# Queries loaded with eight neighbouring tokens of a head pair on a partition

## The chip, the cores and the metric

The kernel runs on one core of a Trainium2 chip. The metric is the time of one execution on the device in microseconds (us). The version before takes 182.44 us, the median of three runs (182.11 to 183.53). The profile comes from one further execution, which took 183.05 us; the span that its trace covers is 181.3 us.

## The reference

A retention recurrence feeds a multiplicative feed-forward network. There are 4 batches, 8 heads, 768 tokens and a head size of 64; the second part takes the 3072 tokens with the heads side by side, 512 wide.

```python
for t in range(S):                       # q, k, v: (4, 8, 768, 64)
    state = gamma[None, :, None, None] * state + einsum('bhd,bhe->bhde', k[:, :, t], v[:, :, t])
    y[:, :, t] = scale * einsum('bhd,bhde->bhe', q[:, :, t], state)
x = y.transpose(0, 2, 1, 3).reshape(B * S, H * D)   # (3072, 512)
h = (x @ w1) * (x @ w2) @ w3                        # 512 -> 1024 -> 1024
out = h @ w_out                                     # (3072, 512), float32
```

## The kernel before

**Tiles.** The tokens are cut into 12 tiles of 256, three to a batch. In each, the recurrence is computed in parallel form: scores of keys against queries, masked to the causal part, times v, plus the queries times the state that came in. Tiles 0 and 1 (`n < EO`) use one layout, tiles 2 to 11 another one with two blocks of 128 tokens. All matrix products are in float16, with float32 sums.

**Loading.** `load` (line 79) brings one tile of q, k or v into a staging buffer of 128 partitions by 1024 float32; there are 15 such buffers. Queries of all tiles, and k and v of tiles 0 and 1, come in one transfer each with two neighbouring tokens of every head on a partition, so each contiguous row is 2 x 64 x 4 = 512 bytes. k and v of later tiles come as two transfers with rows of 256 bytes. Weights come in rows of 4096 bytes. All transfers are issued by SyncE (SP), in one order: the string of names at line 124 (`r` rows of w3, `wo` of w_out, `w1` and `w2`, and q, k, v by tile), then in the tile loop the transposes of tile n+2 (`turns`), the loads of tile n+3 (`loads`), and stores of finished tiles (`STORES`, line 894). A transpose waits for its cast, and whatever stands behind it on SP waits with it.

**Queries.** `cast` (line 269) rounds a staged tile to float16, mostly on GpSimd (POOL), and orders its columns by token within the partition and then by head and feature. The transpose, by TensorE for the first tiles (`turn`) and by a DMA later (`dma_turn`), gives `qT` of shape (128, 2, 4, 128): the partition is a feature of one of two heads, then come the token's parity, the head pair, and the partition that the token was loaded on. A head pair's columns for 32 partitions are thus two contiguous runs of 32 float16.

**Products.** `scores` (lines 331 and 340) multiplies keys by queries, `inter` (line 434) the incoming state by queries, both as 64 by 64 matmuls in four quadrants of the array. `mask` (lines 351 and 357) applies the causal mask, `av` (line 462) adds the product with v. Query columns are in the order of their layout, the even tokens of a block ahead of the odd ones, and so are the tables `keep`, `YS` and `YN`.

**Out of the recurrence.** `x_out` (lines 474 and 482) multiplies by the decay table on VectorE (DVE) and writes `XT`, in which tokens are in their own order again. It is one operation for the first half of the columns and, from tile 2 on, two of 64 partitions for the second, whose two heads have changed places. Its output pattern puts consecutive results of one parity two float16 apart.

**Feed-forward.** w3 @ w_out is folded into `W3O` at the start (line 256). A tile's `two_blocks` (line 497, line 527 for tiles 0 and 1) multiplies W1 and W2 by `XT`; ScalarE (ACT) copies the first product to `pa`, and VectorE multiplies it by the second into `ht` (line 63, with `pa`). `o_unit` (line 545) multiplies by `W3O`, `o_copy` (line 559) scales on ScalarE.

**Order of the work.** Everything is in one order that is written out by hand; each engine does its instructions in that order. Up to tile 3 the order is a list of calls, from line 585 on, with matmuls on zeros (`warm`, line 578) among the first. From tile 4 on a loop gives, for tile n: inter(n), the fences, the last ht of tile n-1, scores and state products of tile n+1, av(n), x_out(n), states and masks of n+1, transposes of n+2, loads and casts of n+3, the two output rows of n-1, then eight blocks of 8 matmuls, W1 and W2 in turn, over three banks of the accumulator memory (`F2`, `F0`, `F1`). The first block is in F2, the second in F0, and the fifth needs F0 again, after the first ht has read it.

Of the kernel before, what the change touches and what calls it, by code (L numbers as in the profile page):

```python
# [21 lines left out]
def kernel(  # L22
# [11 lines left out]
    nc = tc.nc  # L34
# [44 lines left out]
    def load(nm, n, via=None):  # L79
        via = via or nc.sync  # L80
        b, c = divmod(n, PER)
        t = new_stage()
        src = source[nm][b, :, c * T : (c + 1) * T, :]
        if nm == "q" or n < EO:

            via.dma_start(
                t[:, :].rearrange("p (h x) -> p h x", x=2 * D), src.rearrange("h (p t) d -> p h (t d)", t=2)
            )
        else:
            for s in range(2):  # L90
                via.dma_start(
                    t[:, s * 512 : (s + 1) * 512].rearrange("p (h d) -> p h d", d=D),
                    src[:, s * 128 : (s + 1) * 128, :].rearrange("h i d -> i h d"),
                )
        tok_in[nm, n] = t

    def load_rows(src, i):
        t = new_stage()
        nc.sync.dma_start(t[:, :], src[i * 128 : (i + 1) * 128, :])
        return t  # L100

    def load_wo(i):
# [9 lines left out]
    def fetch(names):  # L112
        for x in names.split():
            kind, i = x[:-1], int(x[-1])
            if kind == "r":
                w3_st[i] = load_rows(moe_w3, i)
            elif kind == "wo":
                wo_st[i] = load_wo(i)
            elif kind in ("w1", "w2"):
                w_st[kind, i] = load_rows({"w1": moe_w1, "w2": moe_w2}[kind], i)  # L120
            else:
                load(kind, i)
# [22 lines left out]
    def numbers():  # L145

        nc.gpsimd.iota(key_i[:, :, :], pattern=[[1, 2], [0, H]], base=1 - 128, channel_multiplier=2)
        nc.gpsimd.iota(
            col_i[:, :, :].rearrange("p g (t j) -> p g t j", t=2), pattern=[[128, 2], [1, 2], [2, 64]],
            base=1 - 128, channel_multiplier=0,  # L150
        )

# [13 lines left out]
    def late_numbers():  # L166

        nc.gpsimd.iota(tok_i[:, :, :], pattern=[[128, 2], [0, H]], base=1 - 128, channel_multiplier=1)
        for g in range(2):
            nc.gpsimd.iota(  # L170
                pos_i[:, g, :, :].rearrange("p s (t i) -> p s t i", t=2), pattern=[[128, 2], [1, 2], [2, 32]],
                base=1 - 128 + 64 * g, channel_multiplier=0,
            )

# [58 lines left out]
    def cast_wo(i, eng):  # L233
        copy(eng, WO[i][:, :, :].rearrange("p a n -> p (a n)"), wo_st[i][:, :])

    def cast_w3(f, eng):
        w3h[f] = att.tile([128, 1024], HP, tag="w3h", name="w3h", bufs=5)
        copy(eng, w3h[f][:, :], w3_st[f][:, :])

    def turn_w3(f, tag):  # L240
        src, ps = w3h.pop(f), bank(tag, [128, 1024], HP)
        for g in range(8):
            c0 = g // 2 * 256 + g % 2
            nc.tensor.transpose(ps[:, g * 128 : (g + 1) * 128], src[:, c0 : c0 + 255 : 2], ident16[:, :])
        w3p[f] = ps

    def turned_w3(f, eng):
        w3t[f] = fsb.tile([128, 1024], HP, tag="pa", name="w3t", bufs=8)
        copy(eng, w3t[f][:, :], w3p.pop(f)[:, :])

    def w3_mm(f, i, tag=None, first=False, last=False):
        if first:
            acc[f] = bank(tag, [128, DM])
        for r in range(2):
            g = 2 * i + r
            nc.tensor.matmul(  # L256
                acc[f][:, :], lhsT=w3t[f][:, g * 128 : (g + 1) * 128], rhs=WO[i][:, r, :],
                start=(first and r == 0), stop=(last and r == 1),
            )

# [8 lines left out]
    def cast(nm, n, eng):  # L269
        dst = {"q": q16, "k": k16}[nm]  # L270
        dst[n] = t = att.tile([128, 2, 512], HP, tag=nm + "16", name=nm + "16", bufs=3)
        src = tok_in.pop((nm, n))
        if nm == "q" or n < EO:
            copy(
                eng, t[:, :, :].rearrange("p t (h d) -> p h t d", d=D),
                src[:, :].rearrange("p (h t d) -> p h t d", t=2, d=D),
            )
        else:
            copy(eng, t[:, :, :].rearrange("p s c -> p (s c)"), src[:, :])
# [37 lines left out]

    QUARTERS = ((0, 0), (1, 1), (0, 1), (1, 0))

    def qchunk(n, r, a, s, g):  # L320
        c = 2 * s + g
        return qT[n][half(r), :, a, c * 32 : (c + 1) * 32]

    def scores(n, tags, hp=None):
        if n < EO:
            ps = [bank(t, [128, 2, 2, 128]) for t in tags]
            for i in range(2):
                for t in range(2):
                    for r, g in QUARTERS:
                        a = hp * 2 + i  # L330
                        nc.tensor.matmul(
                            ps[r][half(g), i, t, :], lhsT=kT[n][half(r), t, a, half(g)],
                            rhs=qT[n][half(r), :, a, half(g)], start=True, stop=True,
                        )
        else:
            ps = [bank(t, [128, NP, 2, 64]) for t in tags]
            for a in range(NP):
                for s in range(2):
                    for r, g in QUARTERS:
                        nc.tensor.matmul(  # L340
                            ps[r][half(g), a, s, :], lhsT=kT[n][half(r), s, a, half(g)],
                            rhs=qchunk(n, r, a, s, g), start=True, stop=True,
                        )
        for r in range(2):
            am[n, hp, r] = ps[r]
# [73 lines left out]
    def inter(n, tags):  # L419
        begun = set()  # L420
        for g in range(2):
            X[n, g] = bank(tags[g], [128, NP, 128])
        cs = chunks(n)
        for a in range(NP):
            for c, r in [(c, r) for c in cs for r in range(2)] if n < EO else [
                ((s, g), r) for s in range(2) for g, r in ((0, 0), (1, 1), (0, 1), (1, 0))
            ]:
                if (n, c) in TS:
                    if n < EO:
                        g, o, rhs = c, X[n, c][half(r), a, :], qT[n][half(r), :, a, half(c)]  # L430
                    else:
                        s, g = c
                        o, rhs = X[n, g][place(n, g, r), a, s * 64 : (s + 1) * 64], qchunk(n, r, a, s, g)
                    nc.tensor.matmul(  # L434
                        o, lhsT=TS[n, c][half(r), a, :], rhs=rhs, start=((g, r) not in begun), stop=False,
                        skip_group_check=True,
                    )
                    begun.add((g, r))
        X[n] = begun
# [28 lines left out]
    def x_out(n, g):  # L468
# [3 lines left out]
        if n < EO:  # L472
            order = "p a (t i) -> p a t i"
            nc.vector.tensor_tensor(  # L474
                XT[n][:, :, g * 128 : (g + 1) * 128].rearrange("p a (i t) -> p a t i", t=2),
                x[:, :, :].rearrange(order, t=2), YS[:, g, :, :].rearrange(order, t=2), MULT,
            )
        else:
            xt = XT[n][:, :, :].rearrange("p a (s x) -> p (a s) x", s=2)[:, :, g * 64 : (g + 1) * 64]
            for to in (slice(0, 128),) if g == 0 else (half(0), half(1)):  # L480
                at = to if g == 0 else slice(64 - to.start, 128 - to.start)
                nc.vector.tensor_tensor(  # L482
                    xt[to].rearrange("p k (i t) -> p k t i", t=2),
                    x[at, :, :].rearrange("p a (s t i) -> p (a s) t i", s=2, t=2),
                    YN[at, g, :, :, :].rearrange("p a s (t i) -> p (a s) t i", t=2), MULT,
                )


# [61 lines left out]

    o_sb = {}

    def o_copy(n, tb, c0=0, c1=512):
        if n not in o_sb:
            if n < LAST:
                o_sb[n] = fsb.tile([128, 2, DM], FP, tag="osb", name="osb", bufs=3)[:, :, :]
            else:
                o_sb[n] = new_stage()[:, :].rearrange("p (t c) -> p t c", t=2)
        nc.scalar.activation(o_sb[n][:, tb, c0:c1], o_ps.pop((n, tb, c0, c1))[:, :], AF.Copy, scale=final_scale)  # L559

    def o_store(n, tb, c0=0, c1=512):
        r0 = n * T + tb * 128
# [2 lines left out]
    def o_store_all(n):  # L565
        nc.sync.dma_start(
            out[n * T : (n + 1) * T, :].rearrange("(t p) c -> p t c", t=2), o_sb[n][:, :, :]
        )

    def o_out(n, tb, cuts=((0, 512),)):  # L570
        for c in cuts:
            o_copy(n, tb, *c)
            o_store(n, tb, *c)

    def warm(m, tag="X1"):
        ps = bank(tag, [128, 512])
# [315 lines left out]
    LATE = ()  # L892

    STORES = {6: (2,), 7: (3,), 8: (4,), 9: (5, 0), 10: (6, 7, 1), 11: (8, 9, 10)}
    TVIA = ()
    for n in range(LAST, NS):
        nxt = n + 1 < NS and n > LAST
        late = nxt and n in LATE
        if n > LAST:
# [16 lines left out]
            o_unit(n - 1, 1, ("F0",))  # L916
            o_copy(n - 1, 1)
            for m in STORES.get(n, ()):
                o_store_all(m)
        else:  # L920
            catch_up()
        tags = ("F2", "F0", "X1" if late else "F1")
# [18 lines left out]
                state(n + 1, 5)  # L941
    cuts = ((0, 320), (320, 512))
    o_unit(NS - 1, 0, ("F2",))
    o_out(NS - 1, 0)
    o_unit(NS - 1, 1, ("F0", "F1"), cuts)
    o_out(NS - 1, 1, cuts)


# [28 lines left out]
```

## Time and profile before

| | us |
|---|---|
| median of 3 runs | 182.44 (182.11 to 183.53) |
| the profiled execution, its own time | 183.05 |
| its span in the trace | 181.3 |
| TensorE busy | 174.7 (96%) |
| VectorE busy | 111.5 (61%) |
| ScalarE busy | 68.1 (38%) |
| GpSimd busy | 53.4 (29%) |
| DMA packets on the hardware queue | 83,552, 40.38 MB, 96.2% of 16 engines |
| granted TensorE clock | 1.00 |

The page gives the busy time of each engine over the whole span and the span in 40 slices of 4.5 us. A line of a group has the code line, the engine, the operation, output and inputs by name, the shape and the count; then the busy time, the mean of one in nanoseconds, the idle time ahead of it and what ended that. A line of the timeline begins with its start and its length in us, and ends with the idle time ahead of it, where there was any. Matmuls overlap, so one takes longer from start to end than the distance to the next. SPq is the queue of SyncE: its lines are issues of transfers, and their lengths include the time for which the issue was held.

### The profile page before, as it was taken

The page shows a single profiled execution, that of the slowest core. Times are in us where ns is not written, and L with a number is a line of the kernel's source. Part 1 is how long each engine was busy: PE and PEld are TensorE (multiplying, and loading weights), DVE is VectorE, ACT ScalarE, POOL GpSimd, SP SyncE. Part 2 cuts the span into 40 slices and gives each one's busy share as a digit, 9 for nine tenths or more (in the row PEclk, how much of TensorE's full clock was granted, in tenths as well). Part 3 has the DMA queues.
Part 4 walks back from the last instruction along what each step waited for, and adds up shares of the span by engine and source line. Part 5 has one row for each costly group of instructions (what it writes and reads, how often), then busy time and mean ns, then how long its engine had stood idle before and what let it go on. Part 6 is the DMA issues. An engine that isn't in the chain of part 4 may idle for free.

```text
span 181.3 us, 5987 instructions
## 1 busy us (share of the span) xinstructions
PE 174.7 (96%) x2615; PEld 124.8 (69%) x2615; DVE 111.5 (61%) x212; ACT 68.1 (38%) x123; POOL 53.4 (29%) x55
## 2 busy tenths in 40 slices
PE   7999989899999999999999999999999999999993
PEld 2454645688965685885867858768688587784872
DVE  7541769785775949549469387484674856836330
ACT  8783555620373231323314314232232231331422
POOL 4101243355403254503445343424414410000000
DMA  5999999999999999999999999999999997200303
GB/s 202 348 413 362 347 323 361 409 365 229 215 218 215 207 210 228 118 231 164 237 219 201 219 157 261 216 167 247 267 168 274 157 407 272 94 26 4 116 0 118
DMA packets 83579, 40.76 MB, mean 225 GB/s; under 512 B 61409, under 2 KB 78049, under 8 KB 83553
## 3 DMA queue, kind: packets, MB, share of 16 engines
q1 hardware_dynamic: 83552, 40.38, 96.2%
q8 instruction: 20, 0.33, 0.8%
q14 instruction: 7, 0.05, 0.1%
HBM read 29.36 MB, written 6.29 MB: 197 GB/s over the span
## 4 chain that ended last, share of the span: by engine, by line
PE 91%; DMA 4%; DVE 2%; ACT 1%; issue 1%; ACTq 0%
PE psF L497 35%; PE psF L545 20%; PE psF L578 5%; DMA st<-in_v_dram 4%; PE psX L256 3%; PE psS L527 2%; PE psS L256 2%; PE psX L527 2%; PE psS L545 2%; PE psX L434 2%; PE psS L497 2%; PE psK L527 2%; PE psF L527 2%; PE psX L462 2%; PE psX L497 1%; PE psS L340 1%
## 5 line engine op out<-in xcount | busy, mean ns | idle before, releaser
L497 PEld LDWEIGHTS <-w 128*128 128x128 f16 x640 | 62.6, 98 | 9.4
L497 PE MATMUL psF<-xt,w 128*128 128x256 f16 x576 | 64.4, 273 | 0.0
L63 DVE TENSOR_TENSOR ht<-pa,psF 128x512 f16<-128x512 f32 x39 | 26.7, 685 | 25.8 <-PE psF L497 25.7
L545 PE MATMUL psF<-w3o,ht 128*128 128x512 f16 (+2 forms) x168 | 36.5, 370 | 0.0
L60 ACT COPY pa<-psF 128x512 f32<-128x512 f32 x37 | 21.7, 586 | 33.8 <-PE psF L497 33.8
L545 PEld LDWEIGHTS <-ht 128*128 128x128 f16 x200 | 18.5, 98 | 19.5
L63 POOL TENSOR_TENSOR v<-st,VN 128x1024 f16<-128x1024 f32 x10 | 19.0, 1904 | 21.6 <-DMA st<-in_v_dram 21.6
L482 DVE TENSOR_TENSOR xt<-psX,YN 64x512 f16<-64x512 f32 (+1 forms) x30 | 21.8, 727 | 3.2 <-PE psX L462 2.6
L559 ACT ACTIVATE st<-psF 128x512 f32<-128x512 f32 (+2 forms) x19 | 10.9, 575 | 31.7 <-PE psF L545 31.7
L60 POOL CAST k<-st 128x1024 f16<-128x1024 f32 x8 | 8.3, 1038 | 25.4 <-DMA st<-in_k_dram 20.9
L527 PEld LDWEIGHTS <-w 128*128 128x128 f16 x128 | 12.4, 98 | 2.1 <-issue 0.5
L60 POOL CAST q<-st 128x1024 f16<-128x1024 f32 x9 | 9.4, 1041 | 9.3 <-DMA st<-in_q_dram 7.1
L578 PE MATMUL psF<-zeros 128*128 128x512 f16 x31 | 10.1, 464 | 1.2 <-DVE zeros L132 1.2
L357 DVE TENSOR_TENSOR am<-psS,keep 128x512 f16<-128x512 f32 x16 | 10.2, 680 | 0.8 <-PE psS L340 0.8
L256 PEld LDWEIGHTS <-w3t 128*128 128x128 f16 x64 | 5.7, 98 | 6.0 <-issue 0.3
L256 PE MATMUL psS<-wo,w3t 128*128 128x512 f16 x32 | 8.5, 379 | 0.0
L63 POOL TENSOR_TENSOR t<-s,GS 128x256 f16<-128x256 f32 x8 | 4.9, 614 | 12.1 <-DVE s L63 10.4
L256 PE MATMUL psX<-wo,w3t 128*128 128x512 f16 x32 | 8.4, 380 | 0.0
L60 DVE COPY fence<-psX 128x8 f32<-128x8 f32 x8 | 1.3, 166 | 11.3 <-PE psX L434 11.3
L578 PEld LDWEIGHTS <-zeros 128*128 128x128 f16 x31 | 3.3, 114 | 5.5 <-issue 3.2
L527 PE MATMUL psS<-xt,w 128*128 128x256 f16 x32 | 6.1, 272 | 0.5 <-DVE xt L474 0.5
L60 POOL CAST w<-st 128x1024 f16<-128x1024 f32 x5 | 5.2, 1041 | 4.5 <-DMA st<-in_moe_w_dram 4.5
(131 smaller groups left out, 199.0 us busy)
## 6 DMA issues: line engine op xcount, KB each, us to landing
st<-in_moe_w_dram SPq DMA_DIRECT2D x16, 512.0 KB, 8.2
st<-in_q_dram SPq DMA_DIRECT2D x12, 512.0 KB, 6.7
st<-in_v_dram SPq DMA_DIRECT2D x20, 256.0 KB, 6.0
st<-in_k_dram SPq DMA_DIRECT2D x20, 256.0 KB, 4.9
out_dram<-st SPq DMA_DIRECT2D x8, 512.0 KB, 5.7
st<-in_moe_w_out_dram SPq DMA_DIRECT2D x4, 512.0 KB, 9.9
out_dram<-osb SPq DMA_DIRECT2D x3, 512.0 KB, 5.7
st<-in_k_dram SPq DMA_DIRECT2D x2, 512.0 KB, 9.6
```

The lines of the kernel that those rows point to most:

```text
L60: {"v": nc.vector.tensor_copy, "g": nc.gpsimd.tensor_copy, "s": nc.scalar.copy}[eng](dst, src)
L63: (nc.vector if eng == "v" else nc.gpsimd).tensor_tensor(dst, a, b, op)
L256: nc.tensor.matmul(acc[f][:, :], lhsT=w3t[f][:, g * 128 : (g + 1) * 128], rhs=WO[i][:, r, :], start=(first and r == 0), stop=(last and r = ...
L357: nc.vector.tensor_tensor(t[:, :, :, :].rearrange("p a s i -> p (a s) i"), ps[:, :, :, :].rearrange("p a s i -> p (a s) i"), keep64[:, :]. ...
L434: nc.tensor.matmul(o, lhsT=TS[n, c][half(r), a, :], rhs=rhs, start=((g, r) not in begun), stop=False, skip_group_check=True,)
L462: nc.tensor.matmul(o, lhsT=v16[n][half(g), t, h * D : (h + 1) * D], rhs=rhs, start=((g, r) not in begun), stop=(n >= EO or t == 1), skip_g ...
L482: nc.vector.tensor_tensor(xt[to].rearrange("p k (i t) -> p k t i", t=2), x[at, :, :].rearrange("p a (s t i) -> p (a s) t i", s=2, t=2), YN ...
L497: nc.tensor.matmul(ps[:, i, :], lhsT=W[d][:, f * 128 : (f + 1) * 128], rhs=XT[n][:, d, :], start=(i == 0 and d == 0), stop=(i == 1 and d = ...
L527: nc.tensor.matmul(rows_ps[w, n, uh][j // 2][:, j % 2, :], lhsT=W[d][:, f * 128 : (f + 1) * 128], rhs=XT[n][:, d, :], start=(first and j % ...
L545: nc.tensor.matmul(ps[:, :], lhsT=HT[n][:, f, tb * 128 : (tb + 1) * 128], rhs=W3O[f][:, c0:c1], start=(f == 0), stop=(f == 7),)
L559: nc.scalar.activation(o_sb[n][:, tb, c0:c1], o_ps.pop((n, tb, c0, c1))[:, :], AF.Copy, scale=final_scale)
L578: nc.tensor.matmul(ps[:, :], lhsT=zeros[:, 0:128], rhs=zeros[:, :], start=True, stop=True)
```

## The change

Queries are loaded by four transfers, one for each head pair `a`. Transfer `a` fills the partitions a, a+4, a+8 and so on, with eight neighbouring tokens of both heads of the pair on each: 2 rows of 8 x 64 x 4 = 2048 bytes. The cast orders the columns by token, then by head of the pair and feature. After the transpose, the 128 columns for one of the eight token places are partitions, with head pairs interleaved: a head pair's columns are every fourth one, in eight groups. `queries` is the pattern that picks them. The number tables, and with them the masks and decays, follow the new order of tokens, and `x_out` undoes eight places instead of two, so that consecutive results are eight float16 apart in `XT`.

The stores of tiles 0, 1 and 2 become two transfers of 256 KB each. The number and order of all instructions on TensorE, VectorE, ScalarE and GpSimd stay as they were. On SyncE there are 39 more, each where its single one was. Some helpers gain arguments that keep their old meaning by default; these are left out here.

```diff
 def load(nm, n, via=None):
...
-        if nm == "q" or n < EO:
+        if nm == "q":
+
+            for a in range(NP):
+                via.dma_start(
+                    t[a::NP, :].rearrange("p (r x) -> p r x", r=2),
+                    src[2 * a : 2 * a + 2, :, :].rearrange("r (p t) d -> p r (t d)", t=8),
+                )
+        elif n < EO:
...
-            col_i[:, :, :].rearrange("p g (t j) -> p g t j", t=2), pattern=[[128, 2], [1, 2], [2, 64]],
+            col_i[:, :, :].rearrange("p g (t j) -> p g t j", t=8), pattern=[[128, 2], [1, 8], [8, 16]],
...
-                pos_i[:, g, :, :].rearrange("p s (t i) -> p s t i", t=2), pattern=[[128, 2], [1, 2], [2, 32]],
+                pos_i[:, g, :, :].rearrange("p s (t i) -> p s t i", t=8), pattern=[[128, 2], [1, 8], [8, 8]],
...
 def cast(nm, n, eng):
-        if nm == "q" or n < EO:
+        if nm == "q":
+            copy(
+                eng, t[:, :, :].rearrange("p x c -> p (x c)").rearrange("p (t r d) -> p r t d", t=8, r=2),
+                src[:, :].rearrange("p (r t d) -> p r t d", r=2, t=8),
+            )
+        elif n < EO:
...
+    def queries(n, r, a, i0, i1):
+
+        x = qT[n][half(r), :, :, :].rearrange("p x a i -> p (x a i)").rearrange("p (t i a) -> p t i a", t=8, a=NP)
+        return x[:, :, i0:i1, a]
+
     def qchunk(n, r, a, s, g):
         c = 2 * s + g
-        return qT[n][half(r), :, a, c * 32 : (c + 1) * 32]
+        return queries(n, r, a, c * 8, (c + 1) * 8)
...
-                            rhs=qT[n][half(r), :, a, half(g)], start=True, stop=True,
+                            rhs=queries(n, r, a, 16 * g, 16 * g + 16), start=True, stop=True,
...
-                        g, o, rhs = c, X[n, c][half(r), a, :], qT[n][half(r), :, a, half(c)]
+                        g, o, rhs = c, X[n, c][half(r), a, :], queries(n, r, a, 16 * c, 16 * c + 16)
...
 def x_out(n, g):
-                XT[n][:, :, g * 128 : (g + 1) * 128].rearrange("p a (i t) -> p a t i", t=2),
-                x[:, :, :].rearrange(order, t=2), YS[:, g, :, :].rearrange(order, t=2), MULT,
+                XT[n][:, :, g * 128 : (g + 1) * 128].rearrange("p a (i t) -> p a t i", t=8),
+                x[:, :, :].rearrange(order, t=8), YS[:, g, :, :].rearrange(order, t=8), MULT,
...
-                    xt[to].rearrange("p k (i t) -> p k t i", t=2),
-                    x[at, :, :].rearrange("p a (s t i) -> p (a s) t i", s=2, t=2),
-                    YN[at, g, :, :, :].rearrange("p a s (t i) -> p (a s) t i", t=2), MULT,
+                    xt[to].rearrange("p k (i t) -> p k t i", t=8),
+                    x[at, :, :].rearrange("p a (s t i) -> p (a s) t i", s=2, t=8),
+                    YN[at, g, :, :, :].rearrange("p a s (t i) -> p (a s) t i", t=8), MULT,
...
+    HALVED = (0, 1, 2)
...
             for m in STORES.get(n, ()):
-                o_store_all(m)
+                if m in HALVED:
+                    o_store(m, 0)
+                    o_store(m, 1)
+                else:
+                    o_store_all(m)
```

More of the change, by code (lines that the diff above doesn't have):

```diff
@@ L95, in load, with load_rows @@
         tok_in[nm, n] = t
-    def load_rows(src, i):
+    def load_rows(src, i, c=0, n=1024):
         t = new_stage()
-        nc.sync.dma_start(t[:, :], src[i * 128 : (i + 1) * 128, :])
+        nc.sync.dma_start(t[:, 0:n], src[i * 128 : (i + 1) * 128, c : c + n])
         return t
@@ L115, in fetch @@
             if kind == "r":
-                w3_st[i] = load_rows(moe_w3, i)
+                w3_st[i, None] = load_rows(moe_w3, i)
+            elif kind[0] == "y":
+                w3_st[int(kind[1]), i] = load_rows(moe_w3, int(kind[1]), 512 * i, 512)
             elif kind == "wo":
@@ L234, in cast_wo, with cast_w3, turn_w3, turned_w3 @@
         copy(eng, WO[i][:, :, :].rearrange("p a n -> p (a n)"), wo_st[i][:, :])
[L236 to L242, printed above, removed]
+    def cast_w3(f, eng, z=None):
+        n = 1024 if z is None else 512
+        w3h[f, z] = att.tile([128, 1024], HP, tag="w3h", name="w3h", bufs=5)
+        copy(eng, w3h[f, z][:, 0:n], w3_st[f, z][:, 0:n])
+    def turn_w3(f, tag, z=None):
+        src, ps = w3h.pop((f, z)), bank(tag, [128, 1024], HP)
+        for g in range(8 if z is None else 4):
             c0 = g // 2 * 256 + g % 2
             nc.tensor.transpose(ps[:, g * 128 : (g + 1) * 128], src[:, c0 : c0 + 255 : 2], ident16[:, :])
[L245 to L249, printed above, removed]
+        w3p[f, z] = ps
+    def turned_w3(f, eng, z=None):
+        n = 1024 if z is None else 512
+        w3t[f, z] = t = fsb.tile([128, 1024], HP, tag="pa", name="w3t", bufs=8)
+        copy(eng, t[:, 0:n], w3p.pop((f, z))[:, 0:n])
     def w3_mm(f, i, tag=None, first=False, last=False):
@@ L254, in w3_mm @@
         for r in range(2):
-            g = 2 * i + r
+            src, g = (w3t[f, None], 2 * i + r) if (f, None) in w3t else (w3t[f, i // 2], 2 * (i % 2) + r)
             nc.tensor.matmul(
-                acc[f][:, :], lhsT=w3t[f][:, g * 128 : (g + 1) * 128], rhs=WO[i][:, r, :],
+                acc[f][:, :], lhsT=src[:, g * 128 : (g + 1) * 128], rhs=WO[i][:, r, :],
                 start=(first and r == 0), stop=(last and r == 1),
@@ L551, with o_copy @@
     o_sb = {}
-    def o_copy(n, tb, c0=0, c1=512):
+    def o_copy(n, tb, c0=0, c1=512, eng="s"):
         if n not in o_sb:
@@ L558, in o_copy @@
                 o_sb[n] = new_stage()[:, :].rearrange("p (t c) -> p t c", t=2)
-        nc.scalar.activation(o_sb[n][:, tb, c0:c1], o_ps.pop((n, tb, c0, c1))[:, :], AF.Copy, scale=final_scale)
+        dst, src = o_sb[n][:, tb, c0:c1], o_ps.pop((n, tb, c0, c1))[:, :]
+        if eng == "s":
+            nc.scalar.activation(dst, src, AF.Copy, scale=final_scale)
+        else:
+            nc.vector.tensor_scalar_mul(dst, src, final_scale)
     def o_store(n, tb, c0=0, c1=512):
@@ L568, in o_store_all @@
         )
[L570 to L573, printed above, removed]
     def warm(m, tag="X1"):
@@ L918 @@
             for m in STORES.get(n, ()):
-                o_store_all(m)
+                if m in HALVED:
+                    o_store(m, 0)
+                    o_store(m, 1)
+                else:
+                    o_store_all(m)
         else:
@@ L943 @@
     o_unit(NS - 1, 0, ("F2",))
-    o_out(NS - 1, 0)
+    o_copy(NS - 1, 0)
+    o_store(NS - 1, 0)
     o_unit(NS - 1, 1, ("F0", "F1"), cuts)
-    o_out(NS - 1, 1, cuts)
+    for c, eng in zip(cuts, "ss"):
+        o_copy(NS - 1, 1, *c, eng=eng)
+        o_store(NS - 1, 1, *c)
 _INS = ['q', 'k', 'v', 'moe_w1', 'moe_w2', 'moe_w3', 'moe_w_out']
```

## The prediction

> **What bounds the kernel now.** I read the page's totals and slices first, then its chain, then the timeline of one tile in the steady part, then the groups by shape, and last the start, where transfers matter.
>
> ```profile
> PE 174.7 (96%) x2615; PEld 124.8 (69%) x2615; DVE 111.5 (61%) x212; ACT 68.1 (38%) x123; POOL 53.4 (29%) x55
> PE   7999989899999999999999999999999999999993
> DMA  5999999999999999999999999999999997200303
> PE 91%; DMA 4%; DVE 2%; ACT 1%; issue 1%; ACTq 0%
> ```
>
> Two rows are full: TensorE to the end, the DMA engines for four fifths of the span. The chain settles which one sets the time: 91% of it is TensorE, 4% a DMA. Making transfers cheaper is therefore worth only what TensorE waits for them. The part that decides is what a tile does on VectorE:
>
> ```profile
> 92.72 0.59 PE L462 MATMUL psX<-am,v 64*64 64x64 f16 x32
> 93.25 3.63 PE L545 MATMUL psF<-w3o,ht 128*128 128x512 f16 x16
> 93.47 2.21 DVE L482 TENSOR_TENSOR xt<-psX,YN 128x512 f16<-128x512 f32 x3 [0.30 <-PE psX L462]
> 95.71 0.42 DVE L60 CAST t<-psK 128x256 f16<-128x256 f32 x1
> 96.71 4.97 PE L497 MATMUL psF<-xt,w 128*128 128x256 f16 x44
> 97.43 1.28 DVE L357 TENSOR_TENSOR am<-psS,keep 128x512 f16<-128x512 f32 x2
> 98.73 0.69 DVE L63 TENSOR_TENSOR ht<-pa,psF 128x512 f16<-128x512 f32 x1
> 100.48 0.69 DVE L63 TENSOR_TENSOR ht<-pa,psF 128x512 f16<-128x512 f32 x1 [1.06 <-PE psF L497]
> ```
>
> This is tile 5. After av (L462) VectorE makes xt in three operations (L482), which end at 95.68. TensorE passes that time with the output rows of the tile before (L545) and needs xt at 96.71, so the three may grow by about 1.05 us together. VectorE then works without a gap until the first ht ends at 99.42. That ht frees the bank that the fifth block of L497 writes; at 0.109 us a matmul (64 in 6.98 us) this begins 32 matmuls after 96.71, at 100.2. Less about 0.07 us of signalling, that slack is 0.70 us: the tightest place of the tile.
>
> **The change, part by part.**
>
> *Writing xt.* The 8-token layout makes the step between consecutive f16 results of an x_out 16 bytes instead of 4. Their number stays: three for each of tiles 2 to 11, two for tiles 0 and 1. The nearest rows are these:
>
> ```profile
> L63 DVE TENSOR_TENSOR ht<-pa,psF 128x512 f16<-128x512 f32 x39 | 26.7, 685 | 25.8 <-PE psF L497 25.7
> L482 DVE TENSOR_TENSOR xt<-psX,YN 64x512 f16<-64x512 f32 x20 | 14.5, 726 | 1.6 <-PE psX L462 1.3
> L482 DVE TENSOR_TENSOR xt<-psX,YN 128x512 f16<-128x512 f32 x10 | 7.3, 729 | 1.6 <-PE psX L462 1.2
> ```
>
> Equal element counts; ht is written in order and takes 685 ns, xt with a 4-byte step 727 ns. No row has a wider step. Call d the addition for one operation. Lower end: d = 0, the 42 ns being a fixed price of any step; a gain has no reason, as nothing is left out. If the 42 ns come from passing over the same memory twice instead of once, eight passes add six more, d = 0.25. Upper end: each write takes a second slot. A slot is 1.0 ns, from 680 ns for 512 elements (L357) and 424 ns for 256 (the states, L63), so d = 0.51. I take 0.38, midway between 0.25 and 0.51, because rows show that a step does cost something, and both ways of scaling it leave zero behind.
>
> What is late next, with the slack of each place from the timeline (end of x_out to the first matmul that reads xt): tile 1 has 0.05 us and two operations: 0.76 - 0.05 = 0.71. Tile 2 has 0.62 and tile 3 has 0.37: 1.14 - 0.62 = 0.52 and 0.77. In tiles 5, 6, 8 and 9 the ht slack of 0.70 rules: 4 x 0.44 = 1.76. Tiles 4, 7 and 10 make one state less, VectorE rests some 0.5 us ahead of ht, and the 1.05 rules: 3 x 0.09 = 0.27. Tile 11 has 1.07: 0.07. Tile 0 lies behind other rows of tile 1: 0. Sum 4.1 us. The same sum is 0 at d = 0, 1.2 at 0.25 and 8.3 at 0.51; it costs more than 2.2 us from d = 0.30 on.
>
> [...]
>
> *Reading queries.* Scores (L331, L340) and inter (L434) now read every fourth column of qT, an 8-byte step, in runs of eight. The trace has no moving operand with a step.
>
> ```profile
> 91.87 0.45 PE L434 MATMUL psX<-qT,t 64*64 64x64 f16 x32
> 92.15 0.46 PE L340 MATMUL psS<-qT,kT 64*64 64x64 f16 x32
> ```
>
> 32 of them start within 0.28 us, 8.75 ns each. A column takes 0.426 ns in L497, so 64 columns take 27.3 ns, and four quadrants side by side could start one each 6.8 ns. Lower end 0. Upper end, every column read twice as slowly: 54.5 / 4 = 13.6 ns, 4.9 ns more for 616 matmuls of 64 columns (3.0 us), and 13.5 ns more for 88 of 128 columns (1.2 us): 4.2 us, all on the path. I take 0, since the present pace is already above what reading needs, and keep 4.2 for the range.
>
> [...]
>
> *Loading queries.* Each 512 KB load becomes four of 128 KB with rows of 2048 bytes instead of 512. Casts that wait show landings:
>
> ```profile
> 17.66 1.04 ACT L60 CAST q<-st 128x1024 f16<-128x1024 f32 x1 [2.08 <-DMA st<-in_q_dram]
> 25.82 0.89 DVE L60 CAST k<-st 128x1024 f16<-128x1024 f32 x1 [1.08 <-DMA st<-in_k_dram]
> 40.20 1.04 POOL L60 CAST w<-st 128x1024 f16<-128x1024 f32 x1 [0.27 <-DMA st<-in_moe_w_dram]
> 41.60 1.04 POOL L60 CAST w<-st 128x1024 f16<-128x1024 f32 x1 [0.36 <-DMA st<-in_moe_w_dram]
> 43.38 1.04 POOL L60 CAST q<-st 128x1024 f16<-128x1024 f32 x1 [0.74 <-DMA st<-in_q_dram]
> ```
>
> A weight load in 4096-byte rows lands 1.4 us after the one before it, a query load 1.78. If 2048-byte rows move nearly like 4096, a load saves 0.35 us (between 0.4 saved and, should the four get in each other's way, 0.9 lost, which is half the present rate). Ahead of k0 and v1 stands one query load, q1. TensorE idles 0.48 us for k0's cast (25.82) and 0.27 us for v1's; q1 makes both land 0.35 to 0.4 earlier, a shift of one stretch, so the gain is 0.4 us, at most 0.75. Later loads land earlier too, but from 36 us on TensorE waits for none: worth 0.
>
> *Issues on SP.* 36 more for queries and three more for the stores of tiles 0, 1 and 2, in halves; an issue that is not held takes 0.4 us (0.38 to 0.44 in the timeline), 1.2 us a tile. A DMA waits for the landing of the eighth before it (q3 went out at 32.51, as w11 landed for the cast of 32.47), and the four fill half of these places. Queued behind them on SP are v and the two transposes of the tile after next. A q transpose issued at 93.89 lands about 4.5 us later, and its scores start at 104: over 5 us of cover, so 0. Without that cover it would be 1.2 us a tile. SP's store issues have the same cover. POOL's casts keep their lengths, since both ends are still runs of 64 elements; the masks and tables only hold other numbers. All 0.
>
> *Sum.* The profiled execution took 183.05 us, a span of 181.3 and 1.75 around it: 183.05 + 4.1 - 0.4 = 186.75. It lies 0.6 above the median of 182.44, to which the prediction is made: 186.1.
>
> **The rivals.**
> - *The early loads decide (not slower).* Place: q1 ahead of k0 and v1; price -0.4 us; it decides while d stays below 0.23 and queries read at full pace, since then all xt growth but that of tiles 1 to 3 is covered. For it: the full DMA row, and the small 42 ns. Against: the 4-byte step does cost. 182.0 us. If a gap of 0.55 us in TensorE at 58.7, put down to issue, goes as well, all waits together give 1.3: 181.1.
> - *Queries read at half pace alone.* For it: two quadrants share each partition. Against: the pace above. 182.44 - 0.4 + 4.2 = 186.2.
> - *Both steps cost*, each at its price: 182.44 - 0.4 + 4.1 + 4.2 = 190.3; with d at its upper end 194.5.
> - *The four transfers get in each other's way.* q1 late by 0.9: k0 and v1 add that to the wait: 183.3. Against: k and v already go as two halves each without a visible gap.
>
> **How the numbers follow.** Forecast 0.54, loads decide 0.22, slow queries alone 0.08, both 0.12, hindered transfers 0.04. One per cent is 1.8 us, about what a measurement of this kernel tells from no change. Of the forecast's 0.54, 0.08 is d below 0.30, within 1%; the other 0.46 with 0.08 and 0.12 make slower 0.66. The loads' 0.22 splits into 0.09 faster, where other waits go along, and 0.13 the same; with 0.08 and 0.04 same is 0.25. The range runs from 181.2, both waits and the gap gone, to 194.5; the forecast's own from 183.2 (d = 0.25) to 190.3 (d = 0.51).
>
> **What would show it.** Right: L482 takes 1.0 to 1.25 us; TensorE idles ahead of L497 for xt or ht in tiles 5, 6, 8 and 9; L434 and L340 still start within 0.28 us; k0's cast starts near 25.4. Wrong: L482 near 727 ns (then 182.0), 32 query matmuls over 0.4 us, or transposes that TensorE waits for.

## The result, and the profile after

The changed kernel takes 258.16 us (median of 4 runs, 257.52 to 258.87), 1.414 times the time before, with a 95% interval of 1.407 to 1.420. The forecast was 186.1 with a range from 181.2 to 194.5: the direction held, the size did not. The profiled execution took 257.99 us, its span 256.2. Line numbers are those of the changed kernel: `x_out` writes at 505 (497 for tiles 0 and 1), `two_blocks` is 520, `inter` 457, `scores` 363, `o_unit` 568.

The page of the kernel after, its totals, slices and chain:

```profile
PE 204.7 (80%) x2615; PEld 140.2 (55%) x2615; DVE 167.7 (65%) x212; ACT 68.0 (27%) x123; POOL 54.4 (21%) x55
...
PE   8999959599929849939949769589489399399495
...
PEclk9999997989976988977989979959979989779889
...
PE 61%; DVE 31%; DMA 2%; issue 2%; ACT 1%; SPq 0%; DVEq 0%
```

The full TensorE row has holes now, one in each tile, and VectorE, 2% of the chain before, makes 31% of it. A second thing was nowhere in the prediction: the granted clock, 1.00 before, has dips all along (0.891 in the mean), and TensorE is busy for 30.0 us more (204.7 - 174.7) with the same 2615 matmuls.

The groups by shape say which instruction grew:

```profile
L520 PE MATMUL psF<-xt,w 128*128 128x256 f16 x576 | 82.6, 318 | 34.5 <-DVE xt L505 34.5
...
L505 DVE TENSOR_TENSOR xt<-psX,YN 64x512 f16<-64x512 f32 x20 | 48.1, 2404 | 1.8 <-PE psX L485 1.5
...
L63 DVE TENSOR_TENSOR ht<-pa,psF 128x512 f16<-128x512 f32 x39 | 26.7, 685 | 35.8 <-PE psF L520 35.8
L505 DVE TENSOR_TENSOR xt<-psX,YN 128x512 f16<-128x512 f32 x10 | 24.2, 2423 | 2.2 <-PE psX L485 2.2
```

ht, with as many elements written in order, stays at 685 ns. xt goes from 727 to 2410 ns, with 64 partitions and with 128 alike. And the matmuls of two_blocks take 318 ns instead of 273 on top of a wait of 34.5 us. One tile of the timeline shows both:

```profile
104.06 0.64 PE L363 MATMUL psS<-qT,kT 64*64 64x64 f16 x32
...
105.15 3.63 PE L568 MATMUL psF<-w3o,ht 128*128 128x512 f16 x16
105.46 7.26 DVE L505 TENSOR_TENSOR xt<-psX,YN 128x512 f16<-128x512 f32 x3 [0.37 <-PE psX L485]
...
112.78 10.01 PE L520 MATMUL psF<-xt,w 128*128 128x256 f16 x64 [4.00 <-DVE xt L505]
```

The three writes take 7.26 us instead of 2.21. TensorE finishes the output rows at 108.78, stands idle for 4.00 us, and then needs 10.01 us for 64 matmuls that took 7.15 before. This is tile 4; tiles 7 and 10 are like it, while tiles 5, 6, 8, 9 and 11 wait as long and need 8.6 to 8.8 us.

The waits of TensorE by releaser give the first half of the account:

```profile
PE psF L520 <- DVE xt L505: 34.5, 9, 4.0
...
PE psS L550 <- DVE xt L497: 6.2, 2, 3.3
...
PE psX L520 <- DVE xt L505: 4.9, 1, 4.9
...
PE psX L568 <- DVE xt L505: 1.0, 1, 1.0
```

Together 46.6 us, against 0.5 before. With the 30.0 us of longer matmuls, and less 1.3 for three short waits that are gone (for k0's cast 0.5, for v1's 0.3, and 0.5 put down to issue), the change is 74.8; the span grew by 256.2 - 181.3 = 74.9. The account closes, and the experiments say what stands behind its two large sums.

### The profile page after: what moved, and what is told of

The parts are those of the page before. It is cut to its first block, busy times and chain, and to the rows that moved or that the text cites. A ratio compares the mean times of both kernels' runs of the same rounds, so it can differ in the third digit from the quotient of the medians.

```text
span 256.2 us, 6053 instructions
## 1 busy us (share of the span) xinstructions
PE 204.7 (80%) x2615; PEld 140.2 (55%) x2615; DVE 167.7 (65%) x212; ACT 68.0 (27%) x123; POOL 54.4 (21%) x55
## 4 chain that ended last, share of the span: by engine, by line
PE 61%; DVE 31%; DMA 2%; issue 2%; ACT 1%; SPq 0%; DVEq 0%
PE psF L520 32%; DVE xt L505 28%; PE psS L269 3%; PE psX L269 3%; DMA st<-in_moe_w_dram 2%; DVE xt L497 2%; PE psF L568 2%; PE psX L457 2%; PE psX L520 2%; PE psS L550 2%; PE psK L550 2%; PE psX L550 2%; PE psS L363 2%; PE psS L520 1%; PE psF L550 1%
## 5 line engine op out<-in xcount | busy, mean ns | idle before, releaser
L520 PE MATMUL psF<-xt,w 128*128 128x256 f16 x576 | 82.6, 318 | 34.5 <-DVE xt L505 34.5
L520 PEld LDWEIGHTS <-w 128*128 128x128 f16 x640 | 72.4, 114 | 61.5 <-DVE xt L505 40.6
L505 DVE TENSOR_TENSOR xt<-psX,YN 64x512 f16<-64x512 f32 (+1 forms) x30 | 72.3, 2410 | 4.0 <-PE psX L485 3.7
L63 POOL TENSOR_TENSOR t<-s,GS 128x256 f16<-128x256 f32 x8 | 6.3, 782 | 80.1 <-DVE s L63 80.1
L550 PEld LDWEIGHTS <-w 128*128 128x128 f16 x128 | 14.1, 111 | 9.7 <-issue 6.6
L550 PE MATMUL psS<-xt,w 128*128 128x256 f16 x32 | 7.1, 309 | 6.2 <-DVE xt L497 6.2
L520 PE MATMUL psX<-xt,w 128*128 128x256 f16 x24 | 5.3, 420 | 4.9 <-DVE xt L505 4.9
L497 DVE TENSOR_TENSOR xt<-psS,YS 128x512 f16<-128x512 f32 x3 | 7.2, 2518 | 1.9 <-ACT qT L60 1.9
```

Of the source, the lines that this page charges most:

```text
L63: (nc.vector if eng == "v" else nc.gpsimd).tensor_tensor(dst, a, b, op)
L497: nc.vector.tensor_tensor(XT[n][:, :, g * 128 : (g + 1) * 128].rearrange("p a (i t) -> p a t i", t=8), x[:, :, :].rearrange(order, t=8), Y ...
L505: nc.vector.tensor_tensor(xt[to].rearrange("p k (i t) -> p k t i", t=8), x[at, :, :].rearrange("p a (s t i) -> p (a s) t i", s=2, t=8), YN ...
L520: nc.tensor.matmul(ps[:, i, :], lhsT=W[d][:, f * 128 : (f + 1) * 128], rhs=XT[n][:, d, :], start=(i == 0 and d == 0), stop=(i == 1 and d = ...
L550: nc.tensor.matmul(rows_ps[w, n, uh][j // 2][:, j % 2, :], lhsT=W[d][:, f * 128 : (f + 1) * 128], rhs=XT[n][:, d, :], start=(first and j % ...
```

## The experiments

The theory after the comparison: the 16-byte step of xt's writes costs 1.68 us an operation; TensorE waits for it some 4 us a tile; standing idle lowers its clock; the query reads at a slower pace cost about 4 us more; loads and issues cost nothing. Rival 1: reads, transfers or issues carry a good part. Rival 2: the short runs of the pattern, not the step, are slow. Rival 3: the clock falls for another reason than idling.

**xt in layout order.** The step is taken out, all else stays.

```diff
-  xt[to].rearrange("p k (i t) -> p k t i", t=8),
+  xt[to],     # xt viewed as p k t i; tiles 0 and 1 likewise
```

> The kernel after, with x_out writing xt in the order in which it reads x (no step between the 2-byte values); the output rows are left in that permuted order within a tile. Loads, casts, transposes, query reads with the 8-byte step and tables are those of after. Theory (the write step of x_out is what costs, and the clock falls because TensorE then idles): x_out's operations 0.69 to 0.73 us instead of 2.41, TensorE's clock back at 1.00, and 184 to 188 us: 182.4, minus 0.4 for the loads, plus about 4 for query reads at half pace. Rival 1 (query reads, the four transfers or SP's longer queue carry a good part of the loss): over 195 us although x_out is short. Rival 2 (the short runs of 8 by 8 by 8 in the pattern, not the step of the write, slow the operation): x_out stays near 2.4 us and the time near 258.

Measured: 185.91 us, 1.0135 times before (1.007 to 1.020), clock 0.999. Of the 75.7 us added, 72 go with this one pattern:

```profile
L506 DVE TENSOR_TENSOR xt<-psX,YN 64x512 f16<-64x512 f32 x20 | 13.8, 688 | 1.8 <-PE psX L485 1.5
```

688 ns is nearly what the in-order ht takes (685). Rival 1 falls but for the 3.5 us that are left. Rival 2 loses ground as well: from tile 2 on the writes still go in runs of eight values, 8 by 8 by 8, only that the eight are now neighbours.

**A different step in each tile**, in the kernel before.

```diff
+ t = {2: 2, 3: 1, 4: 4, 5: 8, 6: 16, 7: 32, 8: 2, 9: 4, 10: 8, 11: 16}[n]
- xt[to].rearrange("p k (i t) -> p k t i", t=2),     # x and YN likewise
+ xt[to].rearrange("p k (i t) -> p k t i", t=t),
```

> The kernel before, with the write step of x_out different from tile to tile: tiles 2 to 11 write with steps of 4, 2, 8, 16, 32, 64, 4, 8, 16 and 32 bytes (t = 2, 1, 4, 8, 16, 32, 2, 4, 8, 16). Only tiles with t = 2 keep the tokens in their order. Wanted is the duration of x_out's 64x512 operation by step. Theory (the distance between written values costs): 0.73 at 2 and 4 bytes, about 2.4 at 16, something between at 8, and 2.4 or more at 32 and 64. Rival 2 (what costs is the length of the runs in the pattern, or the read side's step): the operation has its longest time where the inner run is 2 long (64 bytes) or where the read side turns over most, and 8 bytes is as cheap as 4 or as dear as 16 by no order of the step. The time of the whole lies between before and after: 205 to 235 us.

Measured: 212.63 us in one run. VectorE's timeline has the three writes of tiles 4 to 9 in one line each (8, 16, 32, 64, 4 and 8 bytes):

```profile
81.30 3.91 DVE L483 TENSOR_TENSOR xt<-psX,YN 128x512 f16<-128x512 f32 x3
...
93.97 7.26 DVE L483 TENSOR_TENSOR xt<-psX,YN 128x512 f16<-128x512 f32 x3 [0.32 <-PE psX L462]
...
111.32 6.97 DVE L483 TENSOR_TENSOR xt<-psX,YN 128x512 f16<-128x512 f32 x3 [0.18 <-PE psX L462]
...
128.34 7.34 DVE L483 TENSOR_TENSOR xt<-psX,YN 128x512 f16<-128x512 f32 x3
...
145.62 2.21 DVE L483 TENSOR_TENSOR xt<-psX,YN 128x512 f16<-128x512 f32 x3 [0.15 <-PE psX L462]
...
157.37 3.90 DVE L483 TENSOR_TENSOR xt<-psX,YN 128x512 f16<-128x512 f32 x3 [0.15 <-PE psX L462]
```

A third of each is one operation: 0.74 us at 4 bytes, 1.30 at 8, 2.42 at 16, 2.32 at 32, 2.45 at 64; tile 3, with no step, has 0.69. So the time follows the distance: from 4 to 8 bytes it gains 0.56, from 8 to 16 twice that, 1.12, and from 16 on it stays. Runs go down from 16 to 8, 4 and 2 values in tiles 4 to 7, and the shortest are no dearer than those of 8: rival 2 falls. The same kernel shows the clock. TensorE's blocks in tiles 8, 9 and 10, from its timeline:

```profile
148.86 7.15 PE L498 MATMUL psF<-xt,w 128*128 128x256 f16 x64
...
161.32 7.27 PE L498 MATMUL psF<-xt,w 128*128 128x256 f16 x64 [0.55 <-DVE xt L483]
...
177.23 9.90 PE L498 MATMUL psF<-xt,w 128*128 128x256 f16 x64 [3.88 <-DVE xt L483]
```

After no wait or one of 0.55 us the 64 matmuls take about 7.2 us; after 3.88 us they take 9.90. The five blocks of this kernel that follow a wait of 3.57 us or more take 8.50 to 9.90.

**The wide write alone**, in the kernel before: `t=2` becomes `t=8` in all of x_out's patterns.

```diff
- xt[to].rearrange("p k (i t) -> p k t i", t=2),     # x and the tables likewise
+ xt[to].rearrange("p k (i t) -> p k t i", t=8),
```

> The kernel before, with only x_out's pattern of after (16-byte step of the write, runs of 8 by 8 by 8) in all tiles; loads, casts, query reads and tables are those of before, and the tokens of a tile come out in a wrong order. Theory: x_out 2.40 us, TensorE's clock 0.88 to 0.92, and 250 to 256 us, that is after less about 4 for the query reads. Rival 1 (query reads, four transfers or the SP queue carry a good part): under 240 us. Rival 2 makes no difference here.

Measured: 252.67 us, 1.378 times before (1.371 to 1.385), clock 0.904. TensorE waits for xt 47.0 us in all and is busy for 196.9 us, 22.2 more than before; with the 0.5 us of waiting that was there, 68.7, and the span grew by 68.6. So this edit alone makes 70 us of the 75.7. Most of the wait is this line, which is 34.5 us in the change:

```profile
PE psF L497 <- DVE xt L482: 34.4, 9, 3.9
```

**Work in the wait.** The kernel after, with 16 matmuls on zeros behind the output rows of tiles 4 to 11.

```diff
  for m in STORES.get(n, ()):
      ...
+ warm(16, "F2")
```

> The kernel after, plus 16 more matmuls of 512 columns on zeros in each of the tiles 4 to 11, put where TensorE waits for xt (3.4 us a tile at full clock, against a wait of about 4 us). Theory (the granted clock falls because TensorE stands idle some 4 us in each tile): clock 0.97 or more, two_blocks' matmuls back from 318 to about 275 ns, and 228 to 242 us, so less time with more work. Rival 3 (the clock falls for another reason, such as VectorE's long writes or the load on the chip): clock stays near 0.89 and the time at 255 to 265.

Measured: 242.75 us, 1.322 times before (1.313 to 1.332), with a clock of 0.971 in the profiled execution. More work, 15 us less time. The page's clock row and three pieces of its timeline:

```profile
PEclk9999997979998898999999999999999999999999
```

```profile
103.48 3.63 PE L568 MATMUL psF<-w3o,ht 128*128 128x512 f16 x16
...
106.95 3.62 PE L600 MATMUL psF<-zeros 128*128 128x512 f16 x16
...
111.05 7.16 PE L520 MATMUL psF<-xt,w 128*128 128x256 f16 x64 [0.48 <-DVE xt L505]
```

The row is full from the slice in which the filling begins and dips only in the tiles ahead of it, which were not filled. The writes of xt are as long as before the filling (2421 ns), so rival 3 falls: not VectorE's writes but TensorE's idle time lowers its clock (0.891 without the filling, 0.971 with it). The time lies 0.75 us above the upper end of what was expected: the first tiles keep their waits of 3 to 4 us.

In the kernel after, the granted clock falls to 0.50 in twelve stretches, one in each tile, of 3.41 us or of twice that. Each begins 2.9 to 4.7 us after TensorE has gone idle, in the last 1.5 us of the wait or up to 1.2 us behind it. Waits of 2.97 and 3.25 us, in tiles 1 and 0, already bring the clock down. One of 0.55 us, in the kernel with a different step in each tile, costs next to nothing (0.1 us), and waits of 3.6 to 4.0 us cost 1.3 to 2.9 us in the block behind them.

**The step on the other side.** The inner loops of the kernel after are exchanged.

```diff
- xt[to].rearrange("p k (i t) -> p k t i", t=8),
+ xt[to].rearrange("p k (i t) -> p k i t", t=8),     # x and YN likewise
```

> The kernel after with the two inner loops of x_out's pattern exchanged: xt is written in the order of its memory, and the 32-byte step is on the side of the reads (x in PSUM and the table in SBUF, both 4-byte values). The same values come out. Theory, first form (only a write with a step is dear): x_out about 0.7 us and 185 to 187 us as in the run with xt in layout order. Second form (a step is dear on whichever side it lies): x_out 2.0 us or more and 235 to 260 us.

Measured: 188.82 us in one run, x_out at 1073 ns. Neither form was right: the step costs on the side of the reads too, 0.38 us an operation, but a fifth to a quarter of what it costs on the written side (2410 - 688 = 1.72).

**The query reads alone**, in the kernel before: columns with a step of 8 bytes.

```diff
- return qT[n][half(r), :, a, c * 32 : (c + 1) * 32]
+ return queries(n, r, a, c * 32, (c + 1) * 32)     # (t i a) with a picked
```

> The kernel before, with the query columns of scores and inter read with an 8-byte step (so the columns are those of other tokens and heads), nothing else changed. Theory: 32 matmuls take 0.42 us instead of 0.26 to 0.28, and 185.5 to 187 us (182.4 plus about 4). If the half pace lies beside other work: under 183.5 us.

Measured: 186.37 us, 1.0175 times before (1.014 to 1.021), which is 2.5 to 3.9 us; TensorE is busy for 179.0 us, 4.3 more than before, and 32 matmuls start within 0.47 us (before: 0.28). In TensorE's time the price is the upper end of the prediction, 4.2; in the whole time it is 3.2.

**A longer step in the query reads.** The kernel after, its query columns read in token order, 256 bytes apart.

```diff
- return x[:, :, i0:i1, a]
+ return x[:, :, i0:i1, a].rearrange("p t i -> p i t")     # tables and x_out in token order
```

> The kernel after, with the query columns read in token order by the matmuls (eight neighbouring tokens lie 256 bytes apart), the decay tables in natural order, and x_out with no step on either side. The same values come out. x_out about 0.69 us. If the pace of a query matmul depends only on the step in 16-byte terms, it stays near the 13 ns of after and the time is 185 to 188; if a step of 256 bytes is dearer than one of 8, the 64-column groups take 20 ns or more apiece and the time is 190 to 200.

Measured: 196.39 us in one run; x_out 689 ns. The timeline:

```profile
84.67 1.07 PE L457 MATMUL psX<-qT,t 64*64 64x64 f16 x32
...
85.56 1.08 PE L363 MATMUL psS<-qT,kT 64*64 64x64 f16 x32
```

0.89 us for 32, 27.8 ns each: twice the 0.44 us of the 8-byte step and three times the 0.28 of none.

**The loads alone.** Two runs with xt in layout order and query columns read without a step; they differ in where the rows land.

```diff
- t[a::NP, :]                       # every fourth partition, as in the change
+ t[a * 32 : a * 32 + 32, :]        # first run: neighbouring partitions
```

> The kernel of the run with xt in layout order, with the four head pairs of the queries on neighbouring blocks of 32 partitions instead of every fourth partition: rows of 2048 bytes in four transfers stay, and the matmuls read query columns with a 2-byte step as before the change. The output rows are left in the permuted order. What is left of the change is its loads alone. Theory: 181.8 to 182.6 us, that is before minus 0.4 at most for q1 ahead of k0 and v1; query matmuls at 8 to 9 ns. Rival 1 (four transfers and 39 more issues on SP cost): over 183.5 us.

> The run that was to show the loads alone (four blocks of 32 neighbouring partitions) ended at 188.5, with the queries' 2048-byte packets at 145 ns in the mean against 91 where they go to every fourth partition. This kernel puts every fourth partition back, as in the change, and keeps the rest: xt in layout order, query columns read with a 2-byte step (so they are those of other head pairs). If the placement on partitions made that loss, the packets are back at 91 ns, a 512 KB load of queries takes about 1.35 us of the queue, and the time is 181.7 to 182.7, before minus 0 to 0.8. If four transfers with 2048-byte rows and the longer SP queue cost by themselves: over 184 us.

On neighbouring partitions: 186.43 to 189.42 us in six runs, 1.024 times before (1.019 to 1.029). On every fourth: 181.60 us, 0.9927 times before (0.990 to 0.9955). The transfers' own lines, the first run above, the second below:

```profile
st<-in_q_dram SPq DMA_DIRECT2D x48, 128.0 KB, 5.4
```

```profile
st<-in_q_dram SPq DMA_DIRECT2D x48, 128.0 KB, 4.0
```

TensorE's waits come to 9.9 us in the first trace and to 2.0 in the second, and the spans are 187.6 and 179.6. So the placement made the loss, and with the change's own placement the loads save 1.3 us (0.8 to 1.8). The waits of TensorE in the second run are these:

```profile
PE psF L601 <- DVE zeros L141: 1.2, 1, 1.2
PE psS L551 <- DVE xt L497: 0.5, 1, 0.5
PE psX L485 <- ACT fence L60: 0.3, 1, 0.3
```

Those for k0's and v1's casts and the one put down to issue, 0.5, 0.3 and 0.5 us before, are gone: 1.3. Four transfers and 39 issues cost nothing that can be seen.

**Token order restored by TensorE.** inter and av write their columns into PSUM 32 bytes apart, so that x_out has no step.

```diff
- o, lhsT=TS[n, c][half(r), a, :], rhs=rhs, ...
+ o.rearrange("p (i e) -> p e i", e=8), lhsT=TS[n, c][half(r), a, :], rhs=rhs, ...     # av likewise
```

> The kernel after, where inter and av write their columns of x into PSUM in token order (a 32-byte step between the values of a matmul's output), so that x_out has no step on either side, with the decay tables in natural order. The same values come out. x_out 0.69 us. If a step on a matmul's output costs nothing: 185 to 187 us, as in the run with xt in layout order, with 8 to 9 ns for av's matmuls and 13 for inter's. If it costs as a step on the moving operand does: av's 32 matmuls take 0.41 us or more instead of 0.28, 189 us or more.

Measured: 188.18 us, 1.0265 times before (1.023 to 1.031); x_out 689 ns, av's matmuls 13.0 to 13.2 ns apart instead of 8 to 9, inter's 13 as with the step in its reads alone. The second form was nearer: a step on a matmul's output slows it as much, though it is not added to that of the reads.

**Four tokens on a partition**, with the reads of x_out stepped instead of the writes.

```diff
- t[a::NP, :] ... "r (p t) d -> p r (t d)", t=8
+ t[a % 2 :: 2, c0 : c0 + 512] ... "r (p t) d -> p r (t d)", t=4     # c0 = a // 2 * 512
```

> A version between the two kernels: four neighbouring tokens of a head pair on a partition (rows of 1024 bytes, four transfers, two head pairs interleaved on every second partition), so the query columns lie 4 bytes apart; x_out writes in layout order and reads x and the table with a 64-byte step. The same values come out. Wanted are three prices: a query matmul at a 4-byte step (8 to 9 ns if the price begins above it, 13 if any step pays), x_out with four-token reads (0.69 to 1.07 us, between no step and the run with exchanged loops), and a load of 512 KB in 1024-byte rows (1.35 to 1.78 us). If all three are at their low ends, 181.6 to 182.6 us and below the kernel before by up to 1; if query reads pay, 186; if x_out takes 1.07 us, about 3 more.

Measured: 185.27 us, 1.0116 times before (1.008 to 1.015). Query matmuls at the 4-byte step keep their pace of 8.2 to 8.8 ns, so the price of reads begins above 4 bytes. x_out takes 1008 ns, near the upper end: d = 0.28, which by the prediction's slacks is 1.8 us on top of 181.6. The trace shows the other 1.9 us. Against the run with the loads alone, TensorE waits 1.0 us more for casts (k0's 0.5 and v1's 0.3, as before the change, and a weight's 0.2), 2.1 more for xt, and is busy for 0.8 us longer; that makes 3.9, and the spans are 183.5 and 179.6. So with rows of 1024 bytes the two early waits that rows of 2048 bytes removed are back. No kernel here that keeps the tokens' order beats the one before.

## Why the prediction was right or wrong

*The write of xt: the step that failed, by the size of one term.* The prediction took d = 0.38 between 0 and 0.51, its upper end being a second slot for each write. Measured is 1.68 us, 4.4 times the value taken and 3.3 times the upper end. The prediction's slot of 1.0 ns leaves 0.17 us of an operation that do not depend on the count (680 - 512); without them a value takes 2240 / 512 = 4.4 ns, more than four slots where the upper end had two: the price follows the distance up to 16 bytes (0.74 us an operation at 4 bytes, 1.30 at 8, 2.42 at 16), and the 42 ns of the 4-byte step were its hardly visible beginning. No row of before had a second step to extrapolate from, so the two points (in order, 4 bytes) could not bound the third.

*The slacks: right in sum, in part by luck.* With d = 1.68 every slack is used up and the prediction's sum is 32 x 1.68 less the slacks, 8.06: 45.7 us. The waits for xt are 46.6. The slack of 1.05 shows in each of the tiles 4 to 11: 5.04 - 1.05 = 3.99, and they wait 3.9 to 4.0. Two errors nearly cancel: tiles 0 and 1 wait 6.2 us together where the sum has 3.3 for tile 1 and nothing for tile 0, and the 0.35 more that the ht slack gives to each of tiles 5, 6, 8 and 9 is not there as a wait. With d = 0.346 (1073 - 727, the exchanged loops) the same sum is 3.1, and that run lies 2.9 above the one with xt in layout order. There too the total agrees better than its parts: its trace has 1.2 us of waits for xt, only 0.1 more in each block of tiles 5, 6, 8 and 9 where the sum has 0.34, and a gap of 1.0 us put down to issue, which the sum does not hold.

*The clock: a term that was missing.* TensorE's 30.0 us of longer matmuls are 4.3 for the query reads and some 26 for the clock, which is at 0.50 for 54.6 us at the ends of the waits and behind them. The sum treated a wait as its own length; the wait of 4.00 us in tile 4 costs 2.9 more in the block behind it (10.01 us instead of 7.15). No wait in the trace before is longer than 1.2 us, and its clock is 1.00 throughout; at the prediction's own upper end the longest would have been 1.2 (tile 3, 1.53 - 0.37), so this could only come with the mis-sized term.

*The query reads: the wrong end taken.* 0 was taken, 4.2 kept; measured are 4.3 us of TensorE time and 3.2 of the whole. The argument that the present pace leaves room for slower reading did not hold: 32 query matmuls take 0.44 us in the change, over the 0.4 that the prediction named as a sign of being wrong. The runs show 13 to 14 ns a matmul at 8 bytes and 8 to 9 at 4.

*Loads and issues: right in kind, the gain too small.* k0's cast starts at 25.39 (forecast near 25.4), transposes are never waited for, and taken by themselves the loads remove all three waits: the 1.3 us that stood in the first rival as its best case, not the 0.4 of the sum. In the changed kernel the three waits are gone as well, under 75 us of loss.

*What is left over.* The parts measured one by one (69.7 us for the write alone, 3.2 for the reads, less 1.3, by the medians) come to some 72 us, the change to 75.7. TensorE waits for xt for 47.0 us with the write alone and 46.6 with the change, so the rest lies in longer matmuls (204.7 - 196.9 = 7.8, of which the reads make 4.3). The clocks of the two traces (0.904 and 0.891 in the mean) account for it. Each has twelve stretches at 0.50, of 3.41 us or of twice that; four are long in the change (tiles 2, 4, 7 and 10) and two with the write alone. Two more long ones are 6.8 us at half the clock, a loss of 3.4. Why one wait gets a long stretch and another a short one was not tried and stays open.

## What to carry to other kernels

When a layout makes loads cheaper, follow it to the last instruction that undoes it, and count the step in bytes on the side that is written: at 2-byte values the write of VectorE nearly doubles with each doubling of the step from 4 to 16 bytes (0.74, 1.30 and 2.42 us here). Where an engine is 96% busy, as TensorE is here, a new wait can cost more than its length: 2.9 us more behind one of 4.00 us, 0.1 behind one of 0.55. Look at the clock row before pricing what follows. An operation that the trace shows at one step only bounds nothing: the range has to say so.

## What the runs showed of the hardware that was not expected

- VectorE writing 512 float16 values a partition: 0.69 us in order, 0.74 at a 4-byte step, 1.30 at 8, 2.42 at 16, and 2.32 and 2.45 at 32 and 64. Written in order, but with 4-byte values read at a step: 1.07 at 32 bytes, 1.01 at 64.
- TensorE's 64-column matmuls in float16 keep their 8 to 9 ns when the moving operand has a step of 4 bytes; at 8 bytes they take 13 to 14, at 256 25 to 28. An output step of 32 bytes in PSUM makes them 13 as well.
- The queries' 2048-byte packets of the first 60 us take 91 to 92 ns in the mean when a transfer fills every fourth partition, 145 ns when it fills 32 neighbours; the whole time differs by about 6 us.
- TensorE's granted clock falls to 0.50 for 3.41 or 6.83 us at the end of waits of 2.97 to 4.87 us or behind them. Filling its idle time with matmuls on zeros made the changed kernel 15 us faster (242.75 us instead of 258.16).
